# Ten u3 tiles and seven attention outputs turned by transposing DMAs by way of DRAM

## The chip, the cores and the metric

The kernel runs on one core of a Trainium2 chip. The metric is the device time of one execution in microseconds; the number given for a kernel is the median of several runs. TensorE, VectorE, ScalarE and GpSimd each work through their own list of instructions in order; SyncE (SP) issues the DMAs, also in order.

## The reference, cut to what matters

Three stages follow each other in float32: a clustered attention (2 batches, 8 heads, 768 tokens, head size 64), a token and channel mixing network, and a second one with a cosine and sine mixing.

```python
# attention: only tokens of the same cluster see each other
scores = np.where(mask, scale * q @ k.T, -1e9)
attn = softmax(scores)                      # over keys
x = (attn @ v)  -> (B, S, H * D) = (2, 768, 512)
# first mixing
u = x + (relu(x.T @ w_tok1) @ w_tok2).T
x = u + relu(u @ w_ch1) @ w_ch2
# second mixing
theta = x @ w_theta
y = w_tok_r @ (x * cos(theta)) + w_tok_i @ (x * sin(theta))
u = x + y
out = u + relu(u @ w_ch)
```

## The kernel before

Everything stays in SBUF between the stages: xn[0..11] are twelve tiles of 128 tokens x 512 channels (six a batch), first x, then u, then the next x, then the last u. A product of float32 matrices is made of three matmuls (mm3, lines 136 to 142): each operand is split into a high part rounded to float32r and a low part, the difference (split_sb, split_ps).

The attention runs over 48 units: 16 heads of 3 units, each unit 256 queries. In a loop over n, scores() of unit n, turn() of unit n-1 (transposes of the exponentials e) and values() of unit n-2 are written out one after the other. values() leaves the output of two heads of a pair, transposed, in xts[b, pr] (128 channels x 768 tokens). When a pair is complete, exact() (line 86) copies it by DMA into xr, a float32r tile, bit by bit (line 568), and three units later natural() (line 480) turns it into token order with six TensorE transposes against identr, a float32r identity, into PSUM; VectorE multiplies each 128 x 128 block with the reciprocals of the sums into xn (L493). The very last pair is transposed straight from xts against the float32 identity ident. prep() (line 389) copies the split q and k of a pair into the layout of one head, by six DMAs, and place() adds four small ones for the masks (k<-m and q<-m, L385); they go out on SP while the heads before are still at work. GpSimd splits the pairs (split_pair).

In the last stage there are twelve steps, one for each tile (t, b). mix(t, b) makes 36 matmuls and adds into xn. u3_parts(t, b) then copies xn into a float32r tile by DMA (exact, L88). One step later u3_turn makes four TensorE transposes of it against identr into PSUM (L792) and split_ps splits that for the output product; two steps later finish makes twelve matmuls with w_ch, adds, and stores to out. While the steps run, load_tok loads the weights of the next t: each part passes through ScalarE, VectorE and GpSimd (load_w, lines 114 to 134), whose last products are the parts k_h and k_l.

U3_DIRECT is a list of tiles that u3_turn transposes straight from xn against the float32 identity, without the copy; it is empty before. The order of instructions on each engine is planned when the kernel is built, from the order of the code and a timing model.

Of the kernel before, what the change touches and what calls it, by code (L numbers as in the profile page):

```python
# [9 lines left out]
F32 = mybir.dt.float32  # L10
F32R = mybir.dt.float32r
BF16 = mybir.dt.bfloat16
U32 = mybir.dt.uint32
AF = mybir.ActivationFunctionType
ALU = mybir.AluOpType
AX = mybir.AxisListType
PSUM = bass.MemoryType.PSUM

P = 128
BIG = float(2.0**100)  # L20
# [24 lines left out]
X2_COPIED = range(8)  # L45
U_COPIED = (0,)
UT1 = 3
U3_DIRECT = ()
WG = 24
NBLK = 50  # L50
PAIR_AT = (0, 0, 1)
# [5 lines left out]
def tile_model(ctx: ExitStack, tc: tile.TileContext, qT, kT, v, cent, w1, w2, wc1, wc2, wth, wri, wch, out):  # L57


    nc = tc.nc  # L60
    B, H, D, S = qT.shape
    NT = S // P
# [3 lines left out]
    NC = DM // P  # L66
# [8 lines left out]
    marks = {}  # L75
    ident = const.tile([P, P], F32, name="ident")
    make_identity(nc, ident)
    identr = const.tile([P, P], F32R, name="identr")
    nc.vector.tensor_copy(out=identr, in_=ident)
    xn = [const.tile([P, DM], F32, name=f"xn{i}") for i in range(B * NT)]  # L80
    const.tile([P, 96], F32, name="pad")
    halfpi = small.tile([P, 1], F32, name="halfpi")
    nc.gpsimd.memset(halfpi, math.pi / 2)


    def exact(t, x):

        nc.sync.dma_start(out=t.bitcast(F32), in_=x)  # L88
        return t
# [24 lines left out]
    def load_w(src, name, by=None):  # L114

        raw = wpool.tile([P, 512, 2], U32, tag="wraw", bufs=3, name=f"{name}_raw")
        nc.sync.dma_start(out=raw.rearrange("p n t -> p (n t)"), in_=src.bitcast(U32))
# [57 lines left out]
    with ExitStack() as actx:  # L175
        ap = actx.enter_context(tc.tile_pool(name="attn", bufs=1))
        ps_s = actx.enter_context(tc.tile_pool(name="ps_s", bufs=2, space=PSUM))
        ps_t = actx.enter_context(tc.tile_pool(name="ps_t", bufs=3, space=PSUM))
# [9 lines left out]
        def warm_up(n):  # L188
# [17 lines left out]
            out=cs[:, 4:5], in0=cs[:, 0:1], scalar=cs[:, 2:3], in1=cs[:, 1:2], op0=ALU.mult, op1=ALU.add  # L206
# [9 lines left out]
        for j in range(2):  # L216
            r = slice(64 * j, 64 * j + 64)
            dst, src = (t[r, :P].rearrange("p (g a c) -> p g a c", a=2, c=CL)[:, :, j, :] for t in (cst, cps))
# [7 lines left out]
            out=lt, in_=lt, pattern=[[CL, P // CL], [1, CL]], base=0, channel_multiplier=-1,  # L226
# [3 lines left out]
            out=ltri, in_=lt, pattern=[[-CL, P // CL], [0, CL]], base=0, channel_multiplier=1,  # L230
# [171 lines left out]
            return qh, q2[i], k1, k2[i], load_v(b, h)  # L402

        sums = {}
        xts, xrs = {}, {}

        def scores(b, h, u, ops):

# [71 lines left out]
        def natural(b, pr):  # L480

            last = (b, pr) == (B - 1, H // 2 - 1)
            sm, xt = sums[b, pr], (xts if last else xrs)[b, pr]
            ri = small.tile([P, NT, 2], F32, tag="ri", bufs=2, name=f"ri{b}{pr}")
            nc.vector.tensor_scalar(out=ri, in0=sm, scalar1=1e-9, scalar2=None, op0=ALU.add)
            nc.vector.reciprocal(out=ri, in_=ri)
            for q0, n in ((0, 4), (4, 2)):
                ps = ps_t.tile([P, 4, P], F32 if last else F32R, tag="t", name=f"x{b}{pr}{q0}")
                for i in range(n):
                    nc.tensor.transpose(ps[:, i, :], xt[:, (q0 + i) * P : (q0 + i + 1) * P], ident if last else identr)  # L490
                ps = ps.bitcast(F32)
                for i in range(n):
                    nc.vector.tensor_tensor(  # L493
                        out=xn[b * NT + q0 + i][:, pr * P : pr * P + P].rearrange("p (h d) -> p h d", h=2),
                        in0=ps[:, i, :].rearrange("p (h d) -> p h d", h=2),
                        in1=ri[:, q0 + i, :].unsqueeze(2).to_broadcast([P, 2, D]),
                        op=ALU.mult,
                    )
# [15 lines left out]
        late, group = [], []  # L514
        for n in range(len(units) + SKEW):
            if n < len(units):
                b, h, u = units[n]
                if u == 0 and h % 2 == 0:
                    sums[b, h // 2] = small.tile([P, NT, 2], F32, tag="sm", bufs=2, name=f"sm{b}{h}")
                    xts[b, h // 2] = ap.tile([P, S], F32, tag="xt", bufs=2, name=f"xt{b}{h}")  # L520
                if n != 1:
                    es[n] = scores(b, h, u, ops[b, h])
                if n == 0:
                    next(first, None)
                    place(1, ms[0, 0])
                    scored = marks["scores"]
                    es[1] = scores(*units[1], ops[b, h])
                    with tc.issue_after(marks["max"].ins):
                        ops[heads[1]] = prep_first(*heads[1])
                    marks["scores"] = scored  # L530
                    for w, k in zip(WARM[1:], ("cps", "sim", "first", "scores")):
                        with tc.issue_after(marks[k].ins):
                            warm_up(w)
                h1 = n // 3 + 1
                if 1 < h1 < len(heads) and u == PREP[h1 % 2]:
                    b2, h2 = heads[h1]
                    ops[b2, h2] = prep(b2, h2, ms[b2, h2 // 2])
                p1 = n // 6 + 1
                if p1 < len(heads) // 2:
                    pr = heads[2 * p1][0], heads[2 * p1][1] // 2  # L540
                    if n % 6 == PAIR_AT[0]:
                        raws = load_pair(*pr)
                    if n % 6 == PAIR_AT[1]:
                        split_pair(*pr, raws)
                    if n % 6 == PAIR_AT[2]:
                        gen = masks(*pr)
            if n >= 3:
                for _ in range(PACE):
                    next(gen, None)
            if n == 42:  # L550
                mctx.close()
            if 0 <= n - 1 < len(units):
                prs[n - 1] = turn(*units[n - 1], es.pop(n - 1))
            if n < 3:
                with tc.issue_after((marks["turn"] if n else marks["scores"]).ins):
                    for _ in range(PACE):
                        next(gen, None)
            if 0 <= n - SKEW:
                b, h, u = units[n - SKEW]
                group.append((n - SKEW, prs.pop(n - SKEW), ops[b, h][4]))  # L560
                if len(group) == GROUP:
                    with tc.issue_after(marks["turn"].ins):
                        values(group)
                    group = []
                if h % 2 == 1 and u == NT // 2 - 1:
                    late.append((n + 3, b, h // 2))
                    if n - SKEW < len(units) - 1:
                        xrs[b, h // 2] = exact(ap.tile([P, S], F32R, tag="xr", bufs=1, name=f"xr{b}{h}"), xts[b, h // 2])
            while late and (n >= late[0][0] or n == len(units) + SKEW - 1):
                _, b, pr = late.pop(0)  # L570
                natural(b, pr)
            if n in X_AT:
                tok_x(0, X_AT.index(n), part, "pp")
            if n in W1_AT:
                with tc.issue_after(marks["exp"].ins):
                    i = len(w1s)
                    w1s.append(load_w(w1[:, i * 512 : i * 512 + 512], f"w1_{i}", W1_AT[n]))
            if n == len(units):
                with tc.issue_after(marks["tmp"].ins), tc.issue_after(marks["pA"].ins), tc.issue_after(marks["pV"].ins):
                    for i in range(NT // 2):  # L580
                        w2s.append(load_w(w2[:, :, i * 256 : i * 256 + 256], f"w2_{i}", "pv"))


        for t in range(NTT):
            if t == 0:
                ps = ps_s.tile([P, 2, 512], F32, tag="s", name="g00")[:, 0, :]
            else:
                ps = ps_o.tile([P, 512], F32, tag="o", name=f"g0{t}")
# [7 lines left out]
    blk = ctx.enter_context(tc.tile_pool(name="blk", bufs=1, reuse_waits="tile"))  # L596
# [5 lines left out]
    def bank(name):  # L602
        return ps_m.tile([P, 512], F32, tag="mm", name=name)
# [6 lines left out]
    xr = {}  # L610
# [94 lines left out]
    for f0 in range(0, NF - FC, FC):  # L705
        rs, wa = {}, {}
        for f, chs in FIRST if f0 == 0 else LATER:
            if f not in wa:
                a, d = turned[min(f, NCH - 1)] if f0 == 0 and f else split
# [16 lines left out]
    for t in range(B * NT):  # L726
        tick = max(TH0 + TH * t, 8 * (t // 4) + 4 + t % 4 + LAG)
        last = t >= 6
# [35 lines left out]


    wcs = []
    u3 = {}

    def mix(t, b, wts):
        ps = bank(f"y{t}{b}")  # L770
# [9 lines left out]

    def u3_parts(t, b):
        h, l = (blk.tile([P, 512], F32, tag="trig", bufs=8, name=f"u3{k}{t}{b}").bitcast(F32R) for k in "hl")
        u3[t, b] = h, l if (t, b) in U3_DIRECT else exact(l, xn[b * NT + t])

    def u3_turn(t, b):
        if (t, b) in U3_DIRECT:
            u3_parts(t, b)
        h, l = u3[t, b]
        pt = bank(f"u3{t}{b}")
        x, pt, i = (xn[b * NT + t], pt, ident) if (t, b) in U3_DIRECT else (l, pt.bitcast(F32R), identr)  # L790
        for c in range(NC):
            nc.tensor.transpose(pt[:, c * P : c * P + P], x[:, c * P : c * P + P], i)  # L792
        split_ps(h, l, pt)

    def finish(t, b, parts):
# [15 lines left out]
    for n in range(len(steps) + 2):  # L811
        if n < len(steps):
            t, b = steps[n]
# [5 lines left out]
        if n == 0:  # L819
            a, d = marks["x2"]  # L820
# [50 lines left out]
```

## Time and profile before

| | us |
|---|---|
| median of 3 runs | 650.11 (649.92 to 650.73) |
| profiled execution: time | 650.44 |
| profiled execution: span, first to last instruction | 648.7 |
| TensorE busy in the span | 640.5 |
| VectorE busy | 400.6 |
| ScalarE busy | 344.5 |
| GpSimd busy | 257.0 |

The profile is of one execution. The attention takes up to about 245 us, the first mixing network up to about 420, the rest is the second one. The granted TensorE clock has a mean of 0.999. A matmul's end is modelled, so successive ones overlap in the listing: starts, not ends, give the pace.

### The profile page before, as it was taken

How to read it: one execution, taken by the hardware profiler on the slowest of the kernel's cores; microseconds unless marked ns; L12 is line 12 of the kernel's file. 1: busy time of each engine (PE TensorE's matmuls, PEld its weight loads, DVE VectorE, ACT ScalarE, POOL GpSimd, SP SyncE). 2: the span in 40 equal slices, each digit the busy share in tenths (PEclk: the TensorE clock that was granted, in tenths of full speed). 3: DMA queues.
4: the chain of work that ended last, by engine and by line, in shares of the span. 5: the costliest groups of instructions: out<-in, count | busy, mean ns of one | idle time of the engine just before them, and what ended most of it. 6: DMA issues, size and time to landing. Idle time of an engine off the chain costs nothing.

```text
span 648.7 us, 9938 instructions
## 1 busy us (share of the span) xinstructions
PE 640.5 (99%) x3606; PEld 513.0 (79%) x3606; DVE 400.6 (62%) x650; ACT 344.5 (53%) x654; POOL 257.0 (40%) x232
## 2 busy tenths in 40 slices
PE   8999999999999999999999999999999999999997
PEld 6777777777877767888888888878888887888886
DVE  6877787778878758655565522556687856641212
ACT  6767777777778843365434400457587954320000
POOL 7330312319111123057776600532566796550000
PEclk9999999999999999999999999999999999999999
DMA  8665666555655114023443300250121345511111
GB/s 298 169 151 138 175 138 168 132 141 130 141 129 127 58 53 144 31 99 129 131 131 129 116 15 1 72 188 16 51 95 36 98 129 140 184 50 50 49 50 65
DMA packets 28673, 70.48 MB, mean 109 GB/s; under 512 B 4752, under 2 KB 8016, under 8 KB 28624
## 3 DMA queue, kind: packets, MB, share of 16 engines
q1 hardware_dynamic: 28624, 69.85, 37.0%
q8 instruction: 28, 0.46, 0.3%
q14 instruction: 21, 0.17, 0.1%
HBM read 39.65 MB, written 3.15 MB: 66 GB/s over the span
## 4 chain that ended last, share of the span: by engine, by line
PE 54%; POOL 4%; issue 2%; DVE 1%; DMA 1%; ACT 0%; POOLq 0%; DVEq 0%
PE r L140 5%; PE r L141 5%; PE r L142 5%; PE c L140 5%; PE c L142 5%; PE c L141 5%; PE y L141 4%; PE y L142 4%; PE y L140 3%; PE po L140 2%; PE po L141 2%; PE po L142 2%; PE th L140 1%; PE th L142 1%; PE th L141 1%
## 5 line engine op out<-in xcount | busy, mean ns | idle before, releaser
L429 DVE TENSOR_REDUCE nm<-s 128x1 f32<-128x768 f32 x96 | 90.6, 951 | 16.3 <-PE s L427 15.6
L431 ACT ACTIVATE e<-s,nm 128x768 f32<-128x768 f32 x96 | 86.5, 902 | 23.6 <-DVE nm L429 23.3
L446 PE MATMUL t<-ident,e 128*128 128x128 f32 x576 | 84.3, 276 | 0.8 <-ACT e L431 0.4
L446 PEld LDWEIGHTS t<-ident,e 128*128 128x128 f32 x576 | 66.9, 140 | 17.8 <-issue 5.9
L426 PE MATMUL s<-k,qh 128*128 128x384 f32 x188 | 71.7, 381 | 0.6 <-ACT e L431 0.5
L467 PE MATMUL o<-p,vs 128*64 128x256 f32 x564 | 71.2, 388 | 0.0
L449 ACT ACTIVATE p<-t 128x512 f32<-128x512 f32 x96 | 52.8, 595 | 29.1 <-PE t L446 28.9
L427 PE MATMUL s<-k,q 128*128 128x384 f32 x192 | 64.5, 338 | 0.2 <-ACT k L290 0.2
L141 PE MATMUL y<-zh,k_l 128*128 128x512 f32 x144 | 56.1, 390 | 0.5 <-POOL k_l L100 0.5
L142 PE MATMUL r<-uh,c_h 128*128 128x512 f32 x144 | 56.2, 390 | 0.0
L141 PE MATMUL r<-uh,c_l 128*128 128x512 f32 x144 | 56.1, 390 | 0.0
L142 PE MATMUL y<-zh,k_h 128*128 128x512 f32 x144 | 56.1, 390 | 0.0
L140 PE MATMUL y<-zl,k_h 128*128 128x512 f32 x144 | 56.1, 389 | 0.0
L142 PE MATMUL c<-c_h,rh 128*128 128x512 f32 x144 | 56.1, 389 | 0.0
L141 PE MATMUL c<-c_h,rl 128*128 128x512 f32 x144 | 56.0, 389 | 0.0
L140 PE MATMUL c<-c_l,rh 128*128 128x512 f32 x144 | 55.7, 390 | 0.0
L140 PE MATMUL r<-ul,c_h 128*128 128x512 f32 x144 | 55.7, 394 | 0.0
L467 PEld LDWEIGHTS o<-p,vs 128*64 128x64 f32 x564 | 36.3, 136 | 22.9 <-issue 7.1
L130 POOL TENSOR_TENSOR c_f<-c_f,c_raw 128x512 uint32<-128x512 uint32 x24 | 31.8, 1325 | 52.9 <-DVE c_f L127 19.4
L695 ACT ACTIVATE rh<-r 128x512 fp32r<-128x512 f32 x36 | 20.3, 588 | 39.1 <-PE r L142 38.8
L703 DVE TENSOR_TENSOR xn<-c,xn 128x512 f32<-128x512 f32 x36 | 24.3, 685 | 26.3 <-PE c L142 26.2
L94 POOL TENSOR_SCALAR qh<-ql 128x768 fp32r<-128x768 f32 x7 | 5.8, 833 | 85.5 <-DMA qh<-qh 85.3
(201 smaller groups left out, 1403.8 us busy)
## 6 DMA issues: line engine op xcount, KB each, us to landing
c_raw<-wc SPq DMA_DIRECT2D x24, 512.0 KB, 3.3
k_raw<-wri SPq DMA_DIRECT2D x18, 512.0 KB, 3.8
qh<-qh SPq DMA_DIRECT2D x28, 192.0 KB, 3.0
k<-kh SPq DMA_DIRECT2D x28, 192.0 KB, 4.1
ql<-qT SPq DMA_DIRECT2D x8, 384.0 KB, 3.2
kl<-kT SPq DMA_DIRECT2D x8, 384.0 KB, 4.0
vs<-v SPq DMA_DIRECT2D x16, 192.0 KB, 2.4
w_raw<-w SPq DMA_DIRECT2D x6, 512.0 KB, 5.1
```

The lines of the kernel that those rows point to most:

```text
L130: nc.gpsimd.tensor_tensor(out=wu, in0=wu, in1=lo, op=ALU.add)
L140: nc.tensor.matmul(ps, ah, bl, start=first and i == 0, stop=False)
L141: nc.tensor.matmul(ps, al, bh, start=False, stop=False)
L142: nc.tensor.matmul(ps, ah, bh, start=False, stop=last and i == n - 1)
L426: nc.tensor.matmul(ps[:, half, :NH], qh[:, c], k1[:, n], start=True, stop=False)
L427: marks["scores"] = nc.tensor.matmul(ps[:, half, :NH], ql[:, c], kk[:, n], start=False, stop=True)
L429: marks["max"] = nc.vector.tensor_reduce(out=nm, in_=ps[:, :, :NH], axis=AX.XY, op=ALU.max, negate=True)
L431: marks["exp"] = nc.scalar.activation(out=e.rearrange("p (a n) -> p a n", a=2), in_=ps[:, :, :NH], func=AF.Exp, bias=nm, accum_out=sums[b, ...
L446: marks["turn"] = nc.tensor.transpose(ps[:, a, i * P : i * P + P], es[i][:, kt * P : kt * P + P], ident)
L449: marks["pA"] = nc.scalar.activation(out=p, in_=ps, func=AF.Copy)
L467: nc.tensor.matmul(po[r : r + 64, :], vs[:, kt, :], pr[kt // 2][:, kt % 2, :], start=kt < 2, stop=kt >= NT - 2, tile_position=(0, r),)
L703: nc.vector.tensor_tensor(out=xn[t], in0=ps, in1=xn[t], op=ALU.add)
```

## The change

Seven of the eight pairs' outputs and ten of the twelve u3 tiles are no longer transposed by TensorE. A float32 tile is taken as words of two 16-bit halves. halves() copies a tile so that all low halves of a row stand in one plane and all high halves in a second one (GpSimd for a pair, ScalarE and VectorE with a plane each for a u3 tile). store() writes the planes to a DRAM tile; turned_back() reads them with a DMA that transposes 16-bit elements, so that the two halves of each word come to lie beside each other again in the transposed tile. natural() then multiplies from that SBUF tile, at n + 4 where it was n + 3, and split_ps reads it in place of PSUM. The xr tag has two buffers for one. The tiles (0, 0) and (5, 1) are transposed by TensorE straight from xn.

```diff
-U3_DIRECT = ()
+U3_DIRECT = ((0, 0), (5, 1))
...
+    dram = ctx.enter_context(tc.tile_pool(name="dram", bufs=4, space=DRAM))
+
+    def halves(t, x, e):
+
+        o, i = t.bitcast(U16), x.bitcast(U16)
+        n = i.shape[-1] // 2
+        for k, eng in enumerate(e):
+            m = slice(0, 2) if len(e) == 1 else slice(k, k + 1)
+            out = o.rearrange("p (t n) -> p t n", t=2)[:, m]
+            src = i.rearrange("p (n t) -> p t n", t=2)[:, m]
+            if eng == "a":
+                marks["halves"] = nc.scalar.activation(out=out, in_=src, func=AF.Copy)
+            else:
+                marks["halves"] = {"p": nc.gpsimd, "v": nc.vector}[eng].tensor_copy(out=out, in_=src)
+        return t
+
+    def store(rows, t, q):
+
+        q.dma_start(out=rows, in_=t.bitcast(U16).rearrange("p (t n) -> p t n", t=2))
+
+    def turned_back(t, rows, n):
+
+        nc.sync.dma_start_transpose(
+            out=t.bitcast(U16).rearrange("p (c q) -> p c q", c=n), in_=rows.rearrange("p t n -> (p t) n")
+        )
...
@@ natural
-                ps = ps_t.tile([P, 4, P], F32 if last else F32R, tag="t", name=f"x{b}{pr}{q0}")
-                for i in range(n):
-                    nc.tensor.transpose(ps[:, i, :], xt[:, (q0 + i) * P : (q0 + i + 1) * P], ident if last else identr)
-                ps = ps.bitcast(F32)
+                if last:
+                    ps = ps_t.tile([P, 4, P], F32, tag="t", name=f"x{b}{pr}{q0}")
+                    for i in range(n):
+                        nc.tensor.transpose(ps[:, i, :], xt[:, (q0 + i) * P : (q0 + i + 1) * P], ident)
+                else:
+                    ps = xt.rearrange("p (i n) -> p i n", n=P)[:, q0:, :]
...
@@ the loop over the units
-                    late.append((n + 3, b, h // 2))
+                    late.append((n + 4, b, h // 2))
                     if n - SKEW < len(units) - 1:
-                        xrs[b, h // 2] = exact(ap.tile([P, S], F32R, tag="xr", bufs=1, name=f"xr{b}{h}"), xts[b, h // 2])
+                        k = f"{b}{h}"
+                        t = halves(ap.tile([P, S], F32, tag="xr", bufs=2, name=f"xh{k}"), xts[b, h // 2], "p")
+                        rows = dram.tile([P, 2, S], U16, tag="xd", bufs=2, name=f"xd{k}")
+                        store(rows, t, nc.sync)
+                        stored.append((n + 1, (b, h // 2), rows))
+            if stored and n >= stored[0][0]:
+                _, k, rows = stored.pop(0)
+                xrs[k] = ap.tile([P, S], F32, tag="xr", bufs=2, name=f"xr{k[0]}{k[1]}")
+                turned_back(xrs[k], rows, NT)
...
@@ u3_parts, u3_turn
-        u3[t, b] = h, l if (t, b) in U3_DIRECT else exact(l, xn[b * NT + t])
+        if (t, b) not in U3_DIRECT:
+            x = blk.tile([P, 512], F32, tag="blk", bufs=NBLK, name=f"u3x{t}{b}")
+            halves(x, xn[b * NT + t], "av")
+            rows = dram.tile([P, 2, 512], U16, tag="md", bufs=4, name=f"u3d{t}{b}")
+            store(rows, x, nc.sync)
+            turned_back(x, rows, NC)
+            u3x[t, b] = x
+        u3[t, b] = h, l
...
-        pt = bank(f"u3{t}{b}")
-        x, pt, i = (xn[b * NT + t], pt, ident) if (t, b) in U3_DIRECT else (l, pt.bitcast(F32R), identr)
-        for c in range(NC):
-            nc.tensor.transpose(pt[:, c * P : c * P + P], x[:, c * P : c * P + P], i)
+        if (t, b) in U3_DIRECT:
+            pt = bank(f"u3{t}{b}")
+            for c in range(NC):
+                nc.tensor.transpose(pt[:, c * P : c * P + P], xn[b * NT + t][:, c * P : c * P + P], ident)
+        else:
+            pt = u3x.pop((t, b))
         split_ps(h, l, pt)
```

## Rows read from the trace of the kernel before

**Rows 1.** The page's first line.
```profile
span 648.7 us, 9938 instructions
```
**Rows 2.** Waits of TensorE: waiter, releaser; us in total, times, longest.
```profile
PE s L426 <- ACT e L431: 0.5, 1, 0.5
PE y L141 <- POOL k_l L100: 0.5, 1, 0.5
```
**Rows 3.** Windows: stretch, us, busy (instructions) of PE, PEld, DVE, ACT, POOL, clock, DMA.
```profile
110.00:160.00 50.00, 50.00 (x383) 38.44 (x381) 39.44 (x70) 36.91 (x77) 21.52 (x21) 1.00 0.52 127
...
500.00:545.00 45.00, 44.51 (x203) 36.56 (x202) 31.34 (x46) 31.18 (x55) 34.80 (x28) 1.00 0.39 117
```
**Rows 4.** Timeline of TensorE in the attention: start, us, engine, line, what.
```profile
88.61 0.71 PE L490 MATMUL x<-identr,xr 128*128 128x128 f32 x6
89.15 0.41 PE L446 MATMUL t<-ident,e 128*128 128x128 f32 x2
```
**Rows 5.** Timeline of TensorE, one step of the last stage.
```profile
559.75 0.39 PE L140 MATMUL y<-zl,k_h 128*128 128x512 f32 x1
...
567.92 0.45 PE L792 MATMUL u<-identr,u3l 128*128 128x128 f32 x4
...
571.03 0.39 PE L140 MATMUL y<-zl,k_h 128*128 128x512 f32 x1
```
**Rows 6.** Timeline of TensorE at the last x2 turn, on ident.
```profile
500.01 0.60 PE L654 MATMUL x2t<-ident,xn 128*128 128x128 f32 x4
...
500.91 0.40 PE L142 MATMUL th<-th_h,x2h 128*128 128x512 f32 x1
```
**Rows 7.** Timeline of TensorE at the last u3 turn.
```profile
638.46 0.39 PE L142 MATMUL po<-ch_h,u3h 128*128 128x512 f32 x1
638.96 0.50 PE L792 MATMUL u<-identr,u3l 128*128 128x128 f32 x4
```
**Rows 8.** Groups by line and form: busy us, mean ns of one; idle before, releasers.
```profile
L94 POOL TENSOR_SCALAR qh<-ql 128x768 fp32r<-128x768 f32 x7 | 5.8, 833 | 85.5 <-DMA qh<-qh 85.3 <-issue 0.2
L100 POOL TENSOR_TENSOR ql<-ql,qh 128x768 fp32r<-128x768 f32 x7 | 12.8, 1830 | 0.6 <-DMA q<-ql 0.2 <-POOL qh L94 0.2
...
L98 ACT ACTIVATE c_h<-c_f 128x512 fp32r<-128x512 f32 x12 | 7.6, 631 | 27.9 <-POOL c_f L130 26.0 <-PE r L141 2.0
```
**Rows 9.** Longest wait of GpSimd: us in total, times, longest.
```profile
POOL qh L94 <- DMA qh<-qh: 85.3, 5, 19.2
```
**Rows 10.** DMA: a queue's packets, MB, share; issues, KB each, us to landing.
```profile
q1 hardware_dynamic: 28624, 69.85, 37.0%
...
u3l<-xn SPq DMA_DIRECT2D x12, 256.0 KB, 2.3
out<-o SPq DMA_DIRECT2D x11, 256.0 KB, 2.0
...
xr<-xt SPq DMA_DIRECT2D x7, 384.0 KB, 3.6
```
**Rows 11.** Timeline of SP's queue in the attention.
```profile
104.64 0.55 SPq L88 DMA_DIRECT2D xr<-xt  x1
...
111.29 1.22 SPq L385 DMA_DIRECT2D k<-m  x2
...
131.96 0.55 SPq L88 DMA_DIRECT2D xr<-xt  x1
```
**Rows 12.** Timeline of TensorE where the next even head begins.
```profile
115.93 0.71 PE L490 MATMUL x<-identr,xr 128*128 128x128 f32 x6
...
117.81 0.34 PE L427 MATMUL s<-k,q 128*128 128x384 f32 x1
```
**Rows 13.** Timeline of SP's queue in the last stage.
```profile
613.98 0.47 SPq L88 DMA_DIRECT2D u3l<-xn  x1
...
625.26 0.47 SPq L88 DMA_DIRECT2D u3l<-xn  x1
```
**Rows 14.** The k tiles' DMAs from 100 to 120.
```profile
DMA to landing us min/median/max: 1.8/3.1/4.4
```

More of the change, by code (lines that the diff above doesn't have):

```diff
@@ L13 @@
 U32 = mybir.dt.uint32
+U16 = mybir.dt.uint16
 AF = mybir.ActivationFunctionType
@@ L17 @@
 PSUM = bass.MemoryType.PSUM
+DRAM = bass.MemoryType.DRAM
 P = 128
@@ L404, in tile_model @@
         sums = {}
-        xts, xrs = {}, {}
+        xts, xrs, stored = {}, {}, []
         def scores(b, h, u, ops):
@@ L766, in tile_model @@
     wcs = []
-    u3 = {}
+    u3, u3x = {}, {}
     def mix(t, b, wts):
```

## The prediction, on record before the changed kernel ran

> **What bounds the kernel now.** I read the page's shares first: the span is 648.7 us [rows 1], and TensorE is busy in nearly all of it. That alone says little, because the ends of matmuls are modelled, so I went to what TensorE waited for. The list is short; its largest entries after the warm-up are half a microsecond each [rows 2]: one in the attention (scores behind an exponential) and one in the token mixing (a weight part k_l that GpSimd finished late). Then the windows: in the attention, from 110 to 160, TensorE is busy 50.00 of 50 us while VectorE has 39.44 and ScalarE 36.91; from 500 to 545, GpSimd has 34.80 of 45 and the others some 31 [rows 3]. So the time is TensorE's own work, one instruction behind the other, and a transpose taken off TensorE shortens the span by its place in that queue, as long as nobody else becomes late. The one stretch where somebody nearly is late is 500 to 545: the chain that ends last runs through GpSimd there, up to the k_l wait.
>
> **What leaves TensorE.** (1) Seven pairs in natural(): six transposes each, on identr. They start at 88.61 and the next instruction at 89.15: 0.54 us a pair [rows 4], 7 x 0.54 = 3.8 us. (2) Ten u3 tiles: 36 matmuls of the mixing go from 559.75 to 567.92, 0.227 us each; from the turn at 567.92 to the next mixing at 571.03 it is 3.11 us for the turn and twelve output matmuls; 12 x 0.227 = 2.72, so the turn costs 0.38 [rows 5], and ten cost 3.8 us. (3) The two direct tiles change from identr to the float32 ident. The nearest row is an x2 turn on ident: from 500.01 to the third instruction behind it at 500.91 is 0.90; less two matmuls of 0.227, 0.45 [rows 6]. That is 0.07 more than 0.38, twice: minus 0.14 us. (4) The last tile (5,1) is now read from xn with no copy before it. Today the last output matmul in front of it starts at 638.46 and should pass on at 638.69, but the turn starts at 638.96 [rows 7]: 0.27 us come back. The tile (4,1) goes by DMA and is asked for after that turn.
>
> Sum of what leaves: 3.8 + 3.8 - 0.14 + 0.27 = 7.7 us at most.
>
> **What is added.** (a) For each pair GpSimd copies 1,536 half words a partition in one instruction. No row has a two-byte copy; below is the 768-element one-input copy (833 ns, so 1.7 us for twice as many elements), above it the two-input subtraction (1,830 ns, so 3.7 us) [rows 8]. I take 2.2, nearer to the copy. GpSimd is free then: its next instruction waits up to 19.2 us for prep's copies [rows 9], so the cost is nothing unless it is queued behind that wait. (b) For each u3 tile ScalarE and VectorE copy a plane of 512 elements each, side by side; ScalarE's 128x512 rounding from SBUF takes 631 ns [rows 8], and I take the same for VectorE. (c) Each plain copy (256 KB lands in 2.3 us, 384 KB in 3.6) becomes a store to DRAM and a transposing load. A store of 256 KB to DRAM lands in 2.0 us [rows 10]; for a pair I take 3.6 as of the plain copy. No transposing load is in the trace. Below, it lands like the plain copy: 2.3 and 3.6 us. Above, every run of 512 bytes that it writes is one packet: queue q1 spent 37.0% of 16 engines' 648.7 us on 28,624 packets, 134 ns each [rows 1, 10]; a u3 tile has 128 x 4 = 512 such runs and a pair 128 x 6 = 768, over 16 engines 4.3 and 6.4 us; on top of the plain landing 6.6 and 10.0 us. I take 4 and 6, between the ends, nearer to the lower one, since bytes are the same.
>
> **Are the pairs in time?** Today the copy xr is issued at 104.64, and its transposes run at 115.93, 11.3 us later [rows 11, 12]. natural() moves one unit on; xr copies are six units apart and stand at 104.64 and 131.96, so a unit is 4.55 us [rows 11], and 15.8 us are there. The chain is halves 2.2 + issue 0.5 + store 3.6 + issue 0.5 + transposing load 6 = 12.8; with all upper ends 18.3, with the lower ones 9.9. Late would be VectorE's multiplication L493, and behind it on VectorE the maxima of the next scores. In the likeliest case it is hidden.
>
> **Are the u3 tiles in time?** The copies are issued at 613.98 and 625.26, 11.3 us apart [rows 13]. An ordinary tile is wanted by finish() two steps on: 22 us, against 0.6 + 0.5 + 2.0 + 0.5 + 4 and 1.3 for the split, 8.9 us. The shortest is (4,1): from 625.26 to its output matmuls behind the turn at 638.96 [rows 7, 13] is 13.7 us, some 13 once the gaps go. Hidden, even at the upper end (11.5).
>
> **SP's queue.** It issues in order, so the store waits on it for GpSimd, and the transposing load waits for the store; queued behind them are prep's copies for the next even head. The place can be read: the copies run on both sides of 104.64, the last masks k<-m are issued from 111.29 on, two in 1.22 us, so the second at about 111.9 [rows 11]; landing there takes 1.8 to 4.4, median 3.1 us [rows 14], which is 115.0; the first matmul that reads them (L427 of the next head) starts at 117.81 [rows 12]. Slack 2.8 us. Added on SP: the issue of the transposing load, 0.3 to 1.2; the wait for GpSimd, 0 to 3.7; the wait for the store, 0 to 3.6, as the order falls. If the order places each where it is nearly ready, some 1.5 us are added and nothing is lost; at worst 8.5, which is 5.7 late. Likeliest: 0.
>
> **The stretch 500 to 545.** One removed turn, 0.38, lies before the k_l wait and is lost there, since GpSimd's chain decides. Of the new copies, those of one or two tiles fall into it, 0.63 us on ScalarE and on VectorE, both of which feed GpSimd: 0 to 2.5 us longer. I take 0.8. Loss 1.2.
>
> **How much of the attention's 3.8 arrives?** TensorE has no gaps there, but the scores wait once for an exponential [rows 2], and VectorE is at 79% [rows 3]; hand-overs may eat some. I take 3.0; the ends are 0 and 3.8.
>
> Sum: 3.0 + 3.8 + 0.27 - 0.14 - 1.2 = 5.7 us off. The profiled execution has a span of 648.7 in a time of 650.44; the median shown is 650.11, 1.4 over the span. 648.7 - 5.7 + 1.4 = **644.4**.
>
> **Rivals.** *SP's order costs the attention* (the other side): each of six even heads (4, 6, ..., 14) starts late by what SP gains beyond 2.8 us. It decides from 5.7 / 6 = 0.95 us a head, that is 3.75 us added on SP. At 4.8 us (a full wait for the store and the dear issue) it is 2.0 x 6 = 12 us: 656.4; between, 648 to 656. For it: all of it lies in one in-order queue, in its fullest stretch. Against: the order is planned, and a store not ready can stand behind copies that are. *The transposing load is slow.* With all upper ends a pair is 18.3 - 15.8 = 2.5 us late, seven times 17.5 us on VectorE and then TensorE: 662. It starts to cost at a landing of 9 us. For it: nothing in the trace bounds it hard; against: the bytes are few.
> The Trainium skill is of two minds on this load. Its page "VectorE: DVE Perf Modes", section "The three transpose paths", has 1,309 ns for one 128x128 two-byte transpose by DMA; twelve in a row for a pair would be an estimated 15.7 us in place of my 6, a chain of 22.5 against the 15.8, 6.7 us late seven times, and by that page the kernel would take an estimated 691 us. "Advanced Engine Details and Errata", section "X-Bar Transpose (TRN2)", has such DMAs as fast as plain ones, by which the sum stands as it is. No run here shows either yet.
> *The attention keeps its pace* (other engines' hand-overs bind): 644.4 + 3.0 = 647.4. For it: rows 3's 79% on VectorE, which the new multiplications do not relieve much; against: no gap on TensorE.
>
> **How the numbers follow.** Likeliest, all hidden, 641.8 to 646.8: 0.55. Its lower end is the whole 7.7 (642.4) and one hand-over of 0.5 us more, as each pair no longer takes two of the three PSUM tiles that the turns of e use; its upper end has 1.5 of the attention's 3.8 and a loss of 2.1 in the stretch from 500 on. Attention keeps its pace, 646.8 to 648.5: 0.14. SP's order: 0.22, a quarter of it still below 648.8, a quarter within the bound, the rest above. Slow transposing load: 0.09, slower. A measurement tells about 0.2%, 1.3 us, from no change: 648.8 to 651.4 is "same". Faster 0.55 + 0.14 + 0.05 = 0.74, taken down to 0.71 for what a new kind of DMA may bring; same 0.08; slower 0.21. The range, 641.8 to 653, leaves some 2 in 10 out, nearly all above.
>
> **What would show it.** Right: no L490 rows but the last six; u3 turns for two tiles alone; twelve output matmuls directly behind the mixing, the step 10.9 us instead of 11.3; TensorE's waits still short; the multiplications L493 not waiting for a DMA. SP's order: waits of L426 or L427 for DMA q or k at every second head. Slow load: landings over 9 us and L493 waiting for them. The 500 to 545 stretch: the k_l wait grown from 0.5 us to about 1.7. I would be wrong in the mechanism if TensorE lost the transposes and the attention still took as long without a wait to show for it.

## The result, and the profile after

| | us |
|---|---|
| before, beside the changed kernel | 650.07 (649.92 to 650.73, 4 runs) |
| changed kernel | 656.7 (656.4 to 657.36, 4 runs) |
| ratio | 1.0101 [1.0084, 1.0119] |
| profiled execution: time, span | 657.36, 655.6 |

The kernel became 1.0% slower, and the time lies above the predicted range. Of experiment 8 below, one execution was disturbed (704.78 us); it is left out of that kernel's interval, and its profile is read from a repetition, experiment 9.

Lines moved: in the changed kernel natural()'s multiplication is L523, the matmuls of values() are L495, the additions into xt L504, the maxima L457, the exponentials L459, the scores L454 and L455, the matmuls of mm3 L168 to L170. The new lines are L99 and L101 (halves), L106 (store) and L110 (transposing load).

First the page's first line, then the waits of the changed kernel: TensorE's longest, and the new one of VectorE (us in total, times, longest).

```profile
span 655.6 us, 9777 instructions
...
PE o L495 <- DVE xt L504: 10.2, 6, 4.3
...
DVE xn L523 <- DMA xr<-xd: 13.8, 6, 3.2
```

TensorE, whose largest waits after the warm-up were 0.5 us [rows 2], now waits 10.2 us in six places, all in the attention and all for VectorE's additions into xt. VectorE in turn waits 13.8 us in total, also six times, for the transposing load. The k_l wait of [rows 2] is gone, and no wait for a copy of prep() has come up. The windows of [rows 3], and one short one in the attention (same columns):

```profile
110.00:160.00 50.00, 44.39 (x311) 33.89 (x309) 36.34 (x63) 30.28 (x66) 17.97 (x17) 0.93 0.64 151
152.00:158.00 6.00, 4.52 (x18) 2.91 (x19) 3.90 (x8) 3.23 (x7) 5.83 (x8) 0.50 0.82 180
500.00:545.00 45.00, 45.00 (x209) 37.26 (x209) 34.62 (x53) 34.90 (x63) 36.99 (x30) 1.00 0.25 77
```

From 110 to 160 TensorE did 311 matmuls where it did 383. The granted clock column of the second line reads 0.50: between 152 and 158 TensorE ran at the lower of its two levels (1.2 GHz). From 500 to 545 it is busy all the time; the 209 matmuls there are not the 203 of before, since the last stage now starts 12.3 us later (first y matmul at 518.28, before at 505.94).

Where the wait comes from is seen at one pair, its output complete at 105.42. First VectorE (start, us, what, and in brackets idle time before it and its releaser), then GpSimd, then SP's queue:

```profile
105.00 0.42 DVE L504 TENSOR_TENSOR xt<-o,tmp 64x256 f32<-64x256 f32 x1
...
116.38 0.68 DVE L479 COPY p<-t 128x512 f32<-128x512 f32 x1
119.21 1.30 DVE L523 TENSOR_TENSOR xn<-xr,ri 128x128 f32<-128x128 f32 x6 [2.15 <-DMA xr<-xd]
120.43 0.95 DVE L457 TENSOR_REDUCE nm<-s 128x1 f32<-128x768 f32 x1
121.30 0.40 DVE L504 TENSOR_TENSOR xt<-o,tmp 64x256 f32<-64x256 f32 x1
```
```profile
105.48 1.46 POOL L101 COPY xh<-xt 128x1536 uint16<-128x1536 uint16 x1 [0.86 <-DVE xt L504]
134.25 1.46 POOL L101 COPY xh<-xt 128x1536 uint16<-128x1536 uint16 x1 [0.71 <-DVE xt L504]
168.22 1.46 POOL L101 COPY xh<-xt 128x1536 uint16<-128x1536 uint16 x1 [2.17 <-DVE xt L504]
```
```profile
106.20 1.14 SPq L428 DMA_DIRECT2D qh<-qh  x2
...
109.50 0.93 SPq L428 DMA_DIRECT2D k<-kl  x1
110.53 0.86 SPq L106 DMA_DIRECT2D xd<-xh  x1
112.64 1.18 SPq L413 DMA_DIRECT2D q<-m  x2
115.06 1.43 SPq L110 DMA_TRANSPOSE xr<-xd  x1
116.55 1.21 SPq L413 DMA_DIRECT2D k<-m  x2
```

The halves are ready at 106.94, but the store stands on SP behind six copies of prep() and goes out at 110.53; the transposing load goes out at 115.06, when the store has landed; the multiplication starts at 119.21, 13.8 us after the output was complete (this chain of one pair only happens to equal the total of the six waits). VectorE was free for it at 117.06, 11.6 us after, and waited 2.15 us. Behind the waiting instruction stand the next maximum and the next addition into xt, and for that addition TensorE waits, since values() has one PSUM buffer for o. At the fourth pair the stand was the longest (TensorE):

```profile
148.41 0.82 PE L474 MATMUL t<-ident,e 128*128 128x128 f32 x6
153.48 2.83 PE L495 MATMUL o<-p,vs 128*64 128x256 f32 x12 [4.25 <-DVE xt L504]
156.24 0.69 PE L454 MATMUL s<-k,qh 128*128 128x384 f32 x1
...
158.47 0.43 PE L454 MATMUL s<-k,qh 128*128 128x384 f32 x1
...
160.00 1.52 PE L495 MATMUL o<-p,vs 128*64 128x256 f32 x12
161.45 0.44 PE L454 MATMUL s<-k,qh 128*128 128x384 f32 x1
```

After 4.25 us of standing, twelve value matmuls take 2.76 us (153.48 to 156.24); at full clock the same twelve take 1.45 (160.00 to 161.45). The four scores and six turns behind them take 2.23 us (156.24 to 158.47), and the same work takes 1.53 from 158.47 to 160.00. That is 1.31 + 0.70, some 2 us on top of the stand. In the period from 105.48 to 134.25, whose longest stand is 1.28 us, the clock column reads 1.00. The period at the fourth pair, between two halves copies, is 34.0 us (134.25 to 168.22), against 27.32 between two copies before [rows 11].

The account of the attention: the first u turn stands at 272.8 where it stood at 261.1, 11.7 later. Lost: 10.2 in the L495 waits, 1.7 in three waits of the turns of e (L474) for the copies of p, some 2.0 at the lower clock, together 13.9. Gained: some 3 for the transposes (by experiment 3 against experiment 1). That is 11 net; the other 0.8 is not accounted for.

The DMAs by issue (KB each where listed, median us to landing), to set beside [rows 10], and one step of the last stage, to set beside [rows 5]:

```profile
xd<-xh SPq DMA_DIRECT2D x7, 384.0 KB, 4.5
u3d<-u3x SPq DMA_DIRECT2D x10, 256.0 KB, 2.0
...
u3x<-u3d SPq DMA_TRANSPOSE x10, 3.4
xr<-xd SPq DMA_TRANSPOSE x7, 4.1
```
```profile
567.51 0.39 PE L168 MATMUL po<-ch_l,u3h 128*128 128x512 f32 x1
...
578.39 0.39 PE L168 MATMUL po<-ch_l,u3h 128*128 128x512 f32 x1
```

The transposing loads land in 3.4 and 4.1 us. The step is 10.88 us with no turn in it: the last stage does what was forecast.

### The profile page after: what moved, and what is told of

It reads as the page before. It is cut to its first block, busy times and chain, and to the rows that moved or that the text cites. A ratio compares the mean times of both kernels' runs of the same rounds, so it can differ in the third digit from the quotient of the medians.

```text
span 655.6 us, 9777 instructions
## 1 busy us (share of the span) xinstructions
PE 636.4 (97%) x3524; PEld 509.5 (78%) x3524; DVE 413.2 (63%) x660; ACT 347.3 (53%) x664; POOL 268.3 (41%) x239
## 2 busy tenths in 40 slices
DMA packets 49921, 75.33 MB, mean 115 GB/s; under 512 B 26256, under 2 KB 29520, under 8 KB 49872
## 3 DMA queue, kind: packets, MB, share of 16 engines
q1 hardware_dynamic: 49872, 74.70, 40.7%
## 4 chain that ended last, share of the span: by engine, by line
PE 59%; DMA 1%; DVE 0%; issue 0%
PE r L168 5%; PE r L170 5%; PE r L169 5%; PE y L169 5%; PE y L170 5%; PE y L168 5%; PE c L168 5%; PE c L170 5%; PE c L169 5%; PE po L170 2%; PE po L169 2%; PE th L168 2%; PE po L168 2%; PE th L170 2%; PE th L169 2%; PE h L168 1%
## 5 line engine op out<-in xcount | busy, mean ns | idle before, releaser
L459 ACT ACTIVATE e<-s,nm 128x768 f32<-128x768 f32 x96 | 86.9, 905 | 66.1 <-DVE nm L457 66.1
L457 DVE TENSOR_REDUCE nm<-s 128x1 f32<-128x768 f32 x96 | 90.6, 948 | 29.6 <-PE s L455 28.8
L495 PE MATMUL o<-p,vs 128*64 128x256 f32 x564 | 72.6, 393 | 10.4 <-DVE xt L504 10.2
L474 PE MATMUL t<-ident,e 128*128 128x128 f32 x576 | 79.4, 274 | 1.7 <-ACT p L477 0.9
L474 PEld LDWEIGHTS t<-ident,e 128*128 128x128 f32 x576 | 68.2, 141 | 10.1 <-issue 4.8
L454 PE MATMUL s<-k,qh 128*128 128x384 f32 x188 | 72.9, 388 | 0.1
L455 PE MATMUL s<-k,q 128*128 128x384 f32 x192 | 64.8, 340 | 0.2 <-ACT k L318 0.2
L495 PEld LDWEIGHTS o<-p,vs 128*64 128x64 f32 x564 | 36.8, 138 | 33.0 <-DVE xt L504 13.1
L170 PE MATMUL r<-uh,c_h 128*128 128x512 f32 x144 | 56.2, 390 | 0.0
L170 PE MATMUL c<-c_h,rh 128*128 128x512 f32 x144 | 56.1, 389 | 0.0
L170 PE MATMUL y<-zh,k_h 128*128 128x512 f32 x144 | 56.0, 389 | 0.0
L168 PE MATMUL y<-zl,k_h 128*128 128x512 f32 x144 | 56.0, 390 | 0.0
L168 PE MATMUL r<-ul,c_h 128*128 128x512 f32 x144 | 55.7, 394 | 0.0
L168 PE MATMUL c<-c_l,rh 128*128 128x512 f32 x144 | 55.7, 390 | 0.0
L454 PEld LDWEIGHTS s<-k,qh 128*128 128x128 f32 x188 | 35.6, 189 | 18.2 <-ACT p L477 11.2
```

The source lines that it names most:

```text
L168: nc.tensor.matmul(ps, ah, bl, start=first and i == 0, stop=False)
L170: nc.tensor.matmul(ps, ah, bh, start=False, stop=last and i == n - 1)
L454: nc.tensor.matmul(ps[:, half, :NH], qh[:, c], k1[:, n], start=True, stop=False)
L455: marks["scores"] = nc.tensor.matmul(ps[:, half, :NH], ql[:, c], kk[:, n], start=False, stop=True)
L457: marks["max"] = nc.vector.tensor_reduce(out=nm, in_=ps[:, :, :NH], axis=AX.XY, op=ALU.max, negate=True)
L459: marks["exp"] = nc.scalar.activation(out=e.rearrange("p (a n) -> p a n", a=2), in_=ps[:, :, :NH], func=AF.Exp, bias=nm, accum_out=sums[b, ...
```

## The experiments

The theory tested throughout: natural()'s multiplication stands too early in VectorE's order, in front of instructions that TensorE needs, and waits there for the transposing load. The main rivals: SP's order or the additional DMA traffic delays the attention's own operands; the extra work itself is the cost.

**1. The u3 part alone.** The attention is as before.

```diff
...
@@ natural
...
+                ps = ps_t.tile([P, 4, P], F32 if last else F32R, tag="t", name=f"x{b}{pr}{q0}")
+                for i in range(n):
+                    nc.tensor.transpose(ps[:, i, :], xt[:, (q0 + i) * P : (q0 + i + 1) * P], ident if last else identr)
...
@@ the loop over the units
-                    late.append((n + 4, b, h // 2))
+                    late.append((n + 3, b, h // 2))
...
+                        xrs[b, h // 2] = exact(ap.tile([P, S], F32R, tag="xr", bufs=1, name=f"xr{b}{h}"), xts[b, h // 2])
```

> The u3 part alone; the attention as in the kernel before. Theory A (VectorE waits in order for the transposed pairs, and that is all that is lost): this part still earns its TensorE time, 3.8 + 0.27 - 0.14, so some 646 us (4 under the kernel before), the attention as before. Rival B (transposing DMAs disturb whatever runs beside them): the last stage does not get shorter, 649 to 651 us.

Measured: 644.61 us against 650.21, ratio 0.992 [0.9905, 0.9934]. The u3 part earns 5.6 us, more than its terms (3.8 + 0.27 - 0.14 = 3.9). The k_l wait of 0.49 went as well, and in the same step 0.3 more; 0.6 stands already before the last stage (its first y matmul starts at 505.36 where it was 505.94); 0.5 lies behind the last matmul, from whose start to the end of the span it is 3.38 us where it was 3.85. This last part is not the change's: in experiment 4, whose last stage is the old one, it is 3.35.

**2. The pairs alone.** u3_parts and u3_turn are as before.

```diff
-U3_DIRECT = ((0, 0), (5, 1))
+U3_DIRECT = ()
...
+        u3[t, b] = h, l if (t, b) in U3_DIRECT else exact(l, xn[b * NT + t])
```

> The attention part alone; the last stage as in the kernel before. Theory A: all of the loss is here, 650.1 + 11 = some 661 us, with VectorE waiting for xr by DMA some 14 us in six waits, and the clock low once. If the two parts work on each other, the sum of the two differences is not the whole change's +6.6.

Measured: 660.71, ratio 1.0171 [1.0153, 1.0188], with both waits (the first is TensorE's, the second VectorE's):

```profile
PE o L495 <- DVE xt L504: 10.0, 8, 4.3
...
DVE xn L523 <- DMA xr<-xd: 12.7, 6, 3.3
```

The whole loss comes with the pairs, and it is larger than the whole change's. The two parts do not simply add: -5.6 and +10.5 make +4.9, the whole was +6.6. Some 0.7 of the difference is the step with the k_l wait, which can be saved only once: from one tile's first y matmul to the next it took 12.05 us before, 11.39 here and 10.88 in experiment 1 and in the whole change. The rest was not traced.

**3. The multiplication held back on VectorE.** The order of the issue is tied: natural() may not stand before the last maximum written so far.

```diff
-                natural(b, pr)
+                with tc.issue_after(marks["max"].ins):
+                    natural(b, pr)
```

> The whole change, with natural() held behind the score maxima of its own loop step on VectorE (at n + 4 as written), where the plan had moved it ahead by one to two steps. Theory A: no wait of VectorE for xr, no low clock; the transposes' 3 to 3.8 us of the attention come in as well, 642.5 to 645 us. Rival B (SP's order or the DMA traffic holds the attention): the waits go elsewhere and it stays above 650 us.

Measured: 641.56 (641.42 to 641.98) against 650.21, ratio 0.9873 [0.9857, 0.989]: 15.1 us below the change and 8.65 below before. How many maxima of the scores (L457) stand on VectorE ahead of each pair's multiplication:

```
kernel before    23, 35, 47, 59, 71, 83, 95
changed kernel   22, 34, 46, 58, 71, 82, 95
experiment 3     24, 36, 48, 60, 72, 84, 96
```

One or two places decide. Though natural() is written a unit later in the changed kernel, the plan puts the multiplication one maximum earlier than before at five pairs, and at the same one at two. VectorE's timeline at the pair looked at above (the third), whose output is complete at 102.16 here:

```profile
118.14 0.22 DVE L514 RECIPROCAL ri<-ri 128x12 f32<-128x12 f32 x1
118.39 1.30 DVE L523 TENSOR_TENSOR xn<-xr,ri 128x128 f32<-128x128 f32 x6
```

There is no bracket: nothing is waited for, 16.2 us behind the output. TensorE's longest wait after the warm-up is 0.5 us again. The time lies below the 642.5 to 645 that was expected.

**4. The DMAs made, their result unread.** The kernel before, with the pairs' halves, store and transposing load as in the change added to it, into a tile that nobody reads; the pairs are still transposed by TensorE from a plain copy, and the u3 part is as before. The cut is against the changed kernel.

```diff
+                        xrs[b, h // 2] = exact(ap.tile([P, S], F32R, tag="xr", bufs=1, name=f"xr{b}{h}"), xts[b, h // 2])
...
-                        t = halves(ap.tile([P, S], F32, tag="xr", bufs=2, name=f"xh{k}"), xts[b, h // 2], "p")
+                        t = halves(ap.tile([P, S], F32, tag="xq", bufs=2, name=f"xh{k}"), xts[b, h // 2], "p")
...
-                xrs[k] = ap.tile([P, S], F32, tag="xr", bufs=2, name=f"xr{k[0]}{k[1]}")
-                turned_back(xrs[k], rows, NT)
+                turned_back(ap.tile([P, S], F32, tag="xq", bufs=2, name=f"xq{k[0]}{k[1]}"), rows, NT)
```

> The kernel before, all its transposes on TensorE, and in addition the seven halves on GpSimd, the stores to DRAM and the transposing loads, into tiles that nothing reads. Theory A: nobody waits for them, so 650 us, within 1. Rival B (the DMAs delay prep's copies on SP, or take the rings' time): 2 to 12 us slower, with waits of the scores for DMA q or k at every second head.

Measured: 649.8, ratio 0.9999 [0.999, 1.0009]. TensorE's waits for scores (us in total, times, longest):

```profile
PE s L454 <- ACT e L459: 0.5, 1, 0.5
...
PE s L455 <- ACT k L318: 0.2, 1, 0.2
```

None is for a DMA, and neither is any wait for q or k in the changed kernel's own list. The halves, SP's order (planned anew here, with the store behind prep's copies as in the change) and the traffic cost nothing; the cost is in the waiting reader.

**5. Written two units later.** natural() at n + 6, with a third buffer for the sums that it reads.

```diff
-                    sums[b, h // 2] = small.tile([P, NT, 2], F32, tag="sm", bufs=2, name=f"sm{b}{h}")
+                    sums[b, h // 2] = small.tile([P, NT, 2], F32, tag="sm", bufs=3, name=f"sm{b}{h}")
...
-                    late.append((n + 4, b, h // 2))
+                    late.append((n + (4 if (b, h) == (0, H - 1) else 6), b, h // 2))
```

> The whole change, natural() written at n + 6 in place of n + 4 (the last pair of the first batch stays at n + 4; the sums get a third buffer), with no tie to another instruction. In the planned order VectorE's multiplications still stand behind the 22nd, 34th, 46th, 58th, ... maximum, as in the changed kernel (24th, 36th, ... where they were tied to the maxima). Theory A' (the planned place decides, not the written one): as the changed kernel, 656 to 658 us, with the same six waits. Rival (the written place decides): 641 to 645 us.

Measured: 663.83, ratio 1.0214 [1.0199, 1.0229]: slower still, which no theory had expected. The multiplications stand at the same places of VectorE's order as in the changed kernel (22, 34, 46, 58, 71, 82, 95), and the wait is there:

```profile
DVE xn L523 <- DMA xr<-xd: 12.9, 6, 3.7
```

So the place where it is written is not the place where it runs. The additional 7 us are not in the attention: the first u turn stands at 271.6, 1.2 earlier than in the changed kernel. They came behind it, from matmuls that follow each other more slowly; the next two experiments are about that.

**6. The kernel before, with that third buffer alone.**

```diff
-                    sums[b, h // 2] = small.tile([P, NT, 2], F32, tag="sm", bufs=2, name=f"sm{b}{h}")
+                    sums[b, h // 2] = small.tile([P, NT, 2], F32, tag="sm", bufs=3, name=f"sm{b}{h}")
```

> The kernel before with a third buffer for the small tile sm and nothing else. In e5 that buffer moved the weight tiles by 64 bytes (from a multiple of 512 bytes to 448 beyond one), and its matmuls stood 0.233 us apart in the last stage in place of 0.227. If the address does it: some 2 to 3% of the time from 262 on, 657 to 660 us. If it was anything else in e5: 650 us.

Measured: 657.0, ratio 1.011 [1.0087, 1.0132]. The same window of the first mixing, first of the kernel before, then of this one (columns as in [rows 3]):

```profile
300.00:420.00 120.00, 120.00 (x531) 99.38 (x530) 58.04 (x86) 41.22 (x71) 59.38 (x52) 1.00 0.27 88
```
```profile
300.00:420.00 120.00, 120.00 (x518) 96.93 (x517) 56.89 (x82) 39.15 (x68) 57.82 (x50) 1.00 0.25 87
```

TensorE is busy throughout at a granted clock of 1.00, and does 518 matmuls where it did 531. By the kernel's layout, which no view of the profile shows, the third buffer moves the tiles allocated behind it, the weights' among them, 64 bytes a partition lower, from a multiple of 512 bytes to 448 beyond one: 7 us. Which of the moved tiles matters, and why, was not separated.

**7. Experiment 5 with the tiles moved back** to a multiple of 512 bytes.

```diff
+    small.tile([P, 112], F32, name="pad2")
```

> e5 again (natural() written two steps later, not tied), with 448 more bytes set aside behind the third buffer, so that the weight tiles stand on multiples of 512 bytes as before. Theory A': the place on VectorE is as in the changed kernel, so 655 to 657.5 us and six waits of VectorE for xr. If e5's 663.8 was the written place's doing, it stays above 660; if the written place helps, below 650.

Measured: 656.67, ratio 1.0102 [1.0087, 1.0118], the changed kernel's time, with its wait (the line number is one higher):

```profile
DVE xn L524 <- DMA xr<-xd: 13.2, 6, 3.3
```

Writing natural() later is thus worth nothing, and the 7 us of experiment 5 went with the tiles' place.

**8 and 9. One pair held** (the fourth, with the longest stand), twice the same kernel.

```diff
-                natural(b, pr)
+                with tc.issue_after(marks["max"].ins) if (b, pr) == (0, 3) else nullcontext():
+                    natural(b, pr)
```

> The whole change, with only one of the seven pairs (the last of the first batch, where TensorE stood 4.25 us and the granted clock then read 0.50 for 152 to 158) held behind the maxima of its loop step. If each pair costs its own wait and the low clock is a consequence of the long stop: this pair's period falls from 34.0 to some 28.5, 650 to 652 us in all, and no stretch with a low clock. If the low clock comes of something else it stays.

> e7 once more, for an undisturbed profile: 652 us as there; the held pair's period 28 to 29 us in place of 34.0, the granted clock 1.00 in all of 146 to 180, and waits of VectorE for xr in the five other periods, 2 us each.

Measured: 652.67, ratio 1.0031 [1.0015, 1.0047], and 649.9, ratio 1.0008 [0.9994, 1.0023]. The ten runs of experiment 9 lie between 649.06 and 652.48, so by the two medians one pair of seven gives back 4.0 to 6.8 us (from 656.7) of the 15.1 that all give. The second run's rows: VectorE's remaining wait, and the window in which the stand and the low clock were.

```profile
DVE xn L523 <- DMA xr<-xd: 10.4, 5, 2.2
...
149.00:155.00 6.00, 5.99 (x46) 4.31 (x45) 5.90 (x16) 4.36 (x12) 1.98 (x3) 1.00 0.76 179
```

Without the stand the clock stays at 1.00. The held pair's own period falls from 34.0 to 30.5 us (134.12 to 164.60), not to the 28 to 29 expected, but the next one is shorter too: two periods are 55.86 us long (halves copies from 134.12 to 189.98) where they were 62.3 (134.25 to 196.55). Of the 6.4 saved, 4.0 are waits (5.03 us of them in the changed kernel, 0.99 here). The other 2.4 hold what the lower clock cost; read directly from the changed kernel's rows above, that was 2.0.

**10. The store on GpSimd's queue,** which doesn't stand behind prep's copies.

```diff
-                        store(rows, t, nc.sync)
+                        store(rows, t, nc.gpsimd)
```

> The whole change, only the pairs' stores (and those of the u3 tiles stay on SP) issued from GpSimd's own queue, straight behind the copy of the halves, and not from SP behind prep's copies. The waits on VectorE were 2.2 to 3.2 us, and the store stood 3.6 us on SP. If the late landing comes from that stand: the waits go, 642 to 647 us. If the store's and the load's own landings (4.5 and 4.1 us) are what is late: the waits shrink by less than half and it stays above 652 us.

Measured: 653.52, ratio 1.0059 [1.0037, 1.0081]. VectorE's wait, and SP's queue at the third pair:

```profile
DVE xn L523 <- DMA xr<-xd: 9.0, 6, 2.2
...
112.31 1.18 SPq L413 DMA_DIRECT2D q<-m  x2
113.53 0.59 SPq L413 DMA_DIRECT2D k<-m  x1
114.22 1.43 SPq L110 DMA_TRANSPOSE xr<-xd  x1
```

The wait falls from 13.8 to 9.0, so the store's stand on SP was about a third of it. The rest is not the landings alone: GpSimd issues this pair's store at 106.95, it lands after 4.9 us, at 111.83, and the transposing load, still on SP, goes out only at 114.22, behind copies of masks. Another 2.4 us of SP's queue are thus left in the chain.

**11. The tie, with the transposes still on TensorE.** Experiment 1 with natural() at n + 4 and tied as in experiment 3.

```diff
-                    late.append((n + 3, b, h // 2))
+                    late.append((n + 4, b, h // 2))
...
-                natural(b, pr)
+                with tc.issue_after(marks["max"].ins):
+                    natural(b, pr)
```

> e1 (the u3 part alone, all pairs still transposed by TensorE from the float32r copy), with natural() written at n + 4 and held behind the maxima as in e3. e1 is 644.6 us and e3 641.6; the difference of 3.05 came almost all in the first pair's period, not evenly over the pairs. If it is the transposes taken off TensorE: 644.6 or a little above. If it is the order that the tie makes: 641.6, and the seven pairs' DMAs earn nothing.

Measured: 645.07, ratio 0.9919 [0.9894, 0.9943], as experiment 1 (644.61). The tie by itself earns nothing. What experiment 3 gains over experiments 1 and 11, 3.0 us by the ratios (3.05 and 3.5 by the medians), is what taking the seven pairs' transposes off TensorE is worth.

**12. Experiment 3 with the first u3 tile by DMA too.**

```diff
-U3_DIRECT = ((0, 0), (5, 1))
+U3_DIRECT = ((5, 1),)
```

> All pairs held as in e3, and the first u3 tile (0, 0) sent by DMA as well, so eleven tiles: a TensorE turn of 0.45 us less, 641.1 us if nobody waits for it; above 641.6 if the ScalarE and VectorE copies of that tile delay GpSimd's weight parts in the stretch from 500 to 545.

Measured: 648.47, ratio 0.9976 [0.9966, 0.9986]: 6.9 us above experiment 3. TensorE's wait, two windows, and SP's line:

```profile
PE po L168 <- ACT u3h L131: 3.1, 1, 3.1
...
530.00:535.00 5.00, 1.67 (x5) 1.08 (x6) 2.87 (x4) 2.71 (x5) 3.84 (x4) 0.75 0.81 207
535.00:540.00 5.00, 5.00 (x15) 3.90 (x14) 4.90 (x7) 1.66 (x3) 3.26 (x4) 0.57 0.26 74
...
529.36 2.88 SPq L110 DMA_TRANSPOSE u3x<-u3d  x2
```

The loads of the two first tiles go out together at 529.36, the first tile's split comes too late for its output product, TensorE stands 3.1 us, and the granted clock falls again, with 15 matmuls from 535 to 540 where experiment 3 has 24. For this tile, whose output product comes too soon, the way through DRAM does not pay.

## Why the prediction was wrong

**The step that failed** is "Are the pairs in time?". It compared a chain of 12.8 us with the 15.8 us until the place where natural() is written. The chain was not far off: 13.8 at the pair shown (13.7 to 15.5 at the six pairs that waited), with shorter halves (1.46 for 2.2, below my lower bound of 1.7) and load (4.1 for 6), a longer store (4.5 for 3.6), and 3.6 us of the store standing on SP, which had no term in it. The 15.8 was wrong as a deadline: VectorE reached the multiplication 11.6 us after the output, close to the 11.3 of before [rows 11, 12], because its order is planned and not that of the code. The unit that the prediction added was never there (experiments 5 and 7 show the written place to be without effect; experiment 3, that a place one or two maxima later, with 16.2 us, removes the whole loss). In the place of a hidden chain came an in-order wait: 13.8 us on VectorE in six pairs, 10.2 of it passed to TensorE, and some 2 more at the lower clock.

**The rivals.** "The transposing load is slow" had the right place (multiplications late on VectorE, pair after pair, then TensorE) and the wrong cause: the load lands in 4.1 us, not 9. "SP's order costs the attention" is refuted as written by experiment 4; SP's order has a part (experiment 10), but because the store and the load stand behind prep's copies and not because these come late. "The attention keeps its pace" can't be judged in the change itself; with the wait away, the attention as a whole gets 3 us shorter (experiment 3 against experiment 1), but its steady period hardly does (below). The wait itself was among the signs to look for, but a planned place earlier than the written one was no rival and had no chance.

**The transposing load.** 384 KB land in 4.1 us beside the plain copy's 3.6, 256 KB in 3.4 beside 2.3 [rows 10]; I had taken 6 and 4. That such DMAs are as fast as plain ones, as the Trainium skill's "Advanced Engine Details and Errata", section "X-Bar Transpose (TRN2)", has it, agrees with the trace to within half a microsecond for the pair; for the u3 tile the load is 1.1 us slower. The estimate of 15.7 us from the Trainium skill's "VectorE: DVE Perf Modes", section "The three transpose paths", is far from the 4.1. My upper bound had the packets wrong: the profile's page counts 26,256 packets under 512 bytes where it counted 4,752 before, and the 21,504 more are about twice the 10,496 runs that I reckoned with for all the loads. They were cheap all the same: queue q1 went from 37.0% of 648.7 us to 40.7% of 655.6 with 21,248 packets more, an estimated 20 ns each of one engine's time and not the 134 of the mean packet. The issue on SP was dearer than my range: 1.43 us for a pair (0.3 to 1.2 forecast).

**What was right.** What leaves TensorE in the last stage: steps of 10.88 us with no turn, and the last direct turn follows the matmul before it by 0.23 us instead of 0.50 [rows 7]. The u3 tiles are in time; TensorE has no wait in the last stage. The attention's 3.0 is the amount that experiments 3 and 11 measure, but not for the reason given: the rest is lost without a hand-over that TensorE waits for (below), so the match is in part luck. Wrong in the good direction: the 1.2 us in 500 to 545 were not lost, and the last stage, from its first y matmul to the end of the span, is 5.4 us shorter (142.8 before, 137.4 now) where 2.7 were reckoned.

**Where the transposes' 3.8 us went, and what is left open.** With the wait away the steady period hardly moves, 27.28 against 27.32 us, though six transposes have left it; the rows, of experiment 3 and then of before:

```profile
91.11:118.39 27.28, 27.28 (x205) 20.81 (x201) 21.45 (x39) 19.59 (x43) 7.61 (x6) 1.00 0.69 167
```
```profile
104.64:131.96 27.32, 27.32 (x209) 21.02 (x208) 21.59 (x39) 20.28 (x43) 6.13 (x5) 1.00 0.60 152
```

Summed from each start to the next, the six transposes took 0.55 us of such a period; but its 72 turns of e take 7.97 us now, where they took 7.39. Over the whole attention the 42 transposes took 3.76 us in experiment 1, and in experiment 3 the 576 turns of e take 1.41 us more than there (65.25 against 63.84). TensorE is busy throughout; what has changed is the order in which turns, scores and value matmuls follow each other. So a transpose taken off is not simply worth its place in the queue. That the new order is the cause was not tested. Most of the gain is there early: by the second halves copy, at 74.96, experiment 3 is 2.4 us ahead of the second copy before (77.32), but 201 matmuls start between its first and second copy where 216 did, and only six of the 15 are the transposes. So this is in part only another place of the copy.

Which landing time the planner reckoned with is open: no trace shows it.

## What to carry to other kernels

When a chain of DMAs takes the place of a step, the deadline is not the line where the reader is written but the reader's place in its engine's order, and what stands behind it there. Where a planner makes that order, hold the reader back explicitly: one or two places later turned 656.7 us into 641.56, the fastest version here. A stand of the bounding engine can cost more than its length: behind the 4.25 us here the granted clock was at its lower level, which cost some 2 us more.

## What the runs showed of the hardware that was not expected

- After TensorE stood 4.25 us, its granted clock read 0.50 from 152 to 158, which cost some 2 us more; without the stand it stays at 1.00 (experiment 9). A stand of 3.1 us in experiment 12 was followed by 0.57 from 535 to 540.
- The same matmuls at a clock of 1.00 follow each other every 0.232 us instead of 0.226 (120 us by 518 and by 531 of them) when tiles, the weights' among them, lie 64 bytes a partition lower, at 448 beyond a multiple of 512: 7 us of 650 (experiments 6 and 7).
- A transposing load holds SP's queue for 1.43 us (384 KB) and 1.23 (256 KB), where the plain copies took 0.55 and 0.47 [rows 11, 13].
